# Three parts by turns instead of two for the first two token blocks of a fused recurrence and two-layer expert kernel

## The chip, the cores and the metric

The kernel runs on one core of a Trainium2 chip. The metric is the device time of one execution in microseconds. The engines are named as the profile names them: PE (matmul; PEld is its weight load), DVE (vector), ACT (scalar), POOL (GpSimd) and SP (which issues the transfers).

## The reference, cut to what matters

```python
# 1. a gated recurrence: 4 batches x 8 heads, 768 steps of time, head size 48
f = 1.0 / (1.0 + np.exp(-f_logit))
for t in range(S):
    state = f[:, :, t, :, None] * state + np.einsum('bhd,bhe->bhde', k[:, :, t], v[:, :, t])
    y[:, :, t] = np.einsum('bhd,bhde->bhe', q[:, :, t], state)
x = y.transpose(0, 2, 1, 3).reshape(B * S, H * D)     # 3072 tokens x 384

# 2. a product layer, d_ff = 1536
x = ((x @ w_a) * (x @ w_b)) @ w_out

# 3. four experts, F = 1024 each, weighted by p = domain_probs / sum
out = sum(p[:, e:e+1] * (np.maximum(x @ w1[e], 0) @ w2[e]) for e in range(4))
```

The three weight matrices of layer 2 reach the kernel as 64-bit floats; the kernel turns them into 32-bit ones on the chip.

## The kernel before

The 3072 tokens are cut into six **blocks** of 512 (four batches x 128 steps of time). The work has two phases. Phase A does the recurrence and the product layer, phase B the four experts.

**The recurrence** goes in 24 **steps** s (four per block; block i needs steps 4i to 4i+3). A step loads q, k, f and v (`a_load`), prepares them (`a_exp`, `a_scan`, `a_inv`, `a_hat`), and then does transposes, scores and output on PE (`a_trans`, `a_scores`, `a_out`). For steps below `EARLY` (8 before) `a_inv` does nothing: `a_hat` takes 1/R as exp(-ln R) on ACT and refines it with two DVE instructions (L237, L239) and one on POOL (L238), and half of the score mask goes to ACT and POOL (L275, L276). From `EARLY` on the reciprocal is four DVE instructions a step (L215). `a_out` writes the tokens into `xT[i]`, of which there are two buffers (pool `xp`), and after every second step six small transfers move rows inside `xT` (L338). The tiles of a step share `SLOTS` = 11 buffers.

**The product layer** of a block goes over 12 **column blocks** f of `w_a` and `w_b` (128 columns each). A **unit** (i, o, n, f, fs) is one column block for n tokens of block i from column o: two groups of nine matmuls (`half`, L358), an ACT copy (L486), a DVE product (L491 or L494), and then, after the two groups of the next unit, its share of the output product (`outp`). In the first `WHOLE` units the output product is three full 32-bit matmuls (L369); in the others the operands are split into a high and a low part by ACT and POOL (by ACT and DVE from unit `LATE` = 20 on) and nine matmuls follow (L376). A run of units over the column blocks `fs` collects in three banks, which are emptied into `x2raw` at its end: copied in the first run of a block (L391, L393), added by DVE in a later one (L389).

**The order of units.** `parts` cuts the 12 column blocks into 0 to 8 and 9 to 11 (`H1` = 9). Block 0 takes the first part, then block 1 takes it, then block 0 and block 1 take the second; blocks 2 to 5 take all 12 at once. Block 0 starts with four units of 256 tokens, so there are 74 units: unit 4 is block 0's f = 2, units 5 to 10 its f = 3 to 8, units 11 to 19 are block 1's first part, 20 to 22 block 0's second, 23 to 25 block 1's second, and block 2 begins at unit 26.

**The weights.** `conv_to(k)` makes sure that k of the 18 weight tiles of 128 x 768 are ready (two for each column block and one of `w_out` for each two). One conversion is an ACT instruction (L103), six DVE instructions (L104, L106, L109, L112, L113, L116) and, for 12 of the 18, a split by ACT and POOL (L122 on w). Before unit u the kernel calls `conv_to(w_units(min(NF, f + CA)))`, which is two column blocks ahead of the unit.

**Order.** The program text gives the priority; within phase A's first two blocks a planner orders each engine's instructions by that priority and by when they can start, and for blocks 2 to 5 PE keeps the order of the text. `goal` spreads the operations of the recurrence over the units: the steps of the next block are given out over the first `FRAC` (0.4) of the units that remain until that block, in blocks 0 and 1. Each engine runs its own queue in order, and SP issues every transfer in order.

Of the kernel before, what the change touches and what calls it, by code (L numbers as in the profile page):

```python
# [19 lines left out]
B, H, S, D = 4, 8, 768, 48  # L20
# [4 lines left out]
NF = 12  # L25
# [2 lines left out]
NB = 512  # L28
NBLK = NT // NB
HB = 256  # L30
EARLY = 2 * B

SLOTS = 11
FREE = 3 * B
# [2 lines left out]
AHEAD = 2  # L37
GRP = 2
BUSY = (8, 10, 8, 6)
H1 = 9  # L40
NSUB = 2
CA = 2
FRAC = 0.4
WHOLE = 8
LATE = 20
LIMIT = float(2.0 ** 60)

# [5 lines left out]
def gla_moe_moe_kernel(ctx: ExitStack, tc, qkf, vv, wab, wout, w12, probs, gq, gv, gp, out):  # L53
# [65 lines left out]
    def split(engine, hi, lo, x):  # L119

        nc.scalar.copy(out=hi, in_=x)  # L121
        engine.tensor_tensor(out=lo, in0=x, in1=hi.bitcast(F32), op=ALU.subtract)  # L122

    def x2_split(n, pool, tag, bufs):
        t = pool.tile([128, 2, KC, NB], F32R, tag=tag, name="x2", bufs=bufs)
        r = x2raw.pop(n)
        for o in range(0, NB, HB):
            split(nc.gpsimd, t[:, 0, :, o:o + HB], t[:, 1, :, o:o + HB], r[:, :, o:o + HB])
        x2[n] = t


    def phase_a(actx):
# [12 lines left out]
        def w_fetch(u):  # L145
            f, i = 2 * (u // 3), u % 3
            raws[u] = fetch_w(wout[f // 2] if i == 1 else wab[f + i // 2])

        def w_ready(u):
            f, i = 2 * (u // 3), u % 3  # L150
            raw = raws.pop(u)
            if i == 1:
                dst = wo_all[:, f:f + 2].rearrange("p f c -> p (f c)")
                if wide:
                    to_f32(raw, dst)
                else:
                    nc.scalar.copy(out=dst, in_=raw)
                return
            f += i // 2
            w = to_f32(raw) if wide else raw  # L160
            if f == 0:
                w_pair[0] = wts.tile([128, 2, 2, 2 * DM], F32R, tag="x", name="w01", bufs=1)
            t = w_pair[0][:, f] if f < 2 else wts.tile([128, 2, 2 * DM], F32R, tag="w", name="w")
            split(nc.gpsimd, t[:, 0], t[:, 1], w)
            w_f[f] = t.rearrange("p a (i k c) -> p a i k c", i=2, k=KC)
# [18 lines left out]
        def slot(name):  # L184
            return at.tile([128, 4, C], F32, tag="t", name=name, bufs=SLOTS)
# [27 lines left out]
        def a_inv(s, j):  # L213
            if s >= EARLY:
                nc.vector.reciprocal(out=T[s]["f"][:, j], in_=T[s]["R"][:, j])  # L215

        def a_hat(s):
# [6 lines left out]
            j1 = at.tile([128, 4, C], BF16, tag="j", name="j")  # L224
            if s >= EARLY:
                nc.gpsimd.tensor_tensor(out=k, in0=k, in1=R, op=ALU.mult)  # L226
# [32 lines left out]
        def a_scores(s):  # L259
# [12 lines left out]
            for h in range(2):  # L272
                m = slot("ss")
                if h and s < EARLY:
                    nc.scalar.copy(out=m.rearrange("p j c -> p (j c)"), in_=sps[h])  # L275
# [14 lines left out]
        def a_out(s):  # L290
# [50 lines left out]
            if not last:  # L341
                new = at.tile([128, 4, D], F32, tag="st", name="st", bufs=B + 1)
                uv = ups[:, :4 * D].rearrange("p (j e) -> p j e", j=4)
                pe = t["pe"].to_broadcast([128, 4, D])
                sign = 1.0 if s >= EARLY else -1.0
                if c:
# [6 lines left out]
        def half(i, o, n, f, which):  # L353
            p = bank("h")[:, :n]
            x, w = xT[i], w_f[f]
            ops = [(w[:, a, which, k], x[:, q, k, o:o + n]) for k in range(KC) for a, q in ((0, 0), (0, 1), (1, 0))]
            for m, (l, r) in enumerate(ops):
                kept(nc.tensor.matmul(p, l, r, start=m == 0, stop=m == len(ops) - 1))  # L358
            return p
# [3 lines left out]
        def outp(i, o, n, f, fs, w, hl):  # L363
            if (i, fs[0]) not in x2ps:
                x2ps[i, fs[0]] = [bank("o") for _ in range(KC)]
            banks = x2ps[i, fs[0]]
            for m in range(KC):
                if w is None:
                    nc.tensor.matmul(  # L369
                        banks[m][:, o:o + n], wo_all[:, f, m * 128:(m + 1) * 128], hl,  # L370
                        start=f == fs[0] and o == 0, stop=f == fs[-1], skip_group_check=True,
                    )
                    continue
                for q, (a, b) in enumerate(((0, 0), (0, 1), (1, 0))):

                    kept(nc.tensor.matmul(  # L376
                        banks[m][:, o:o + n], w[:, a, m * 128:(m + 1) * 128], hl[:, b],
                        start=f == fs[0] and q == 0 and o == 0, stop=f == fs[-1] and q == 2, skip_group_check=True,
                    ))
            if f != fs[-1]:  # L380
                return
            old = x2raw.get(i)
            if old is None:
                x2raw[i] = keep.tile([128, KC, NB], F32, tag="k", name="x2raw")
            for c in range(o, o + n, HB):
                for m in range(KC):
                    dst, p = x2raw[i][:, m, c:c + HB], banks[m][:, c:c + HB]
                    if old is not None:
                        nc.vector.tensor_tensor(out=dst, in0=p, in1=dst, op=ALU.add)  # L389
                    elif m == 1:  # L390
                        nc.vector.tensor_copy(out=dst, in_=p)  # L391
                    else:
                        nc.scalar.copy(out=dst, in_=p)  # L393
# [6 lines left out]
        NW = 3 * NF // 2  # L400
        fetch, ready = list(range(NW)), list(range(NW))

        def conv_to(k):

            while len(ready) > max(0, NW - k):
                w_ready(ready.pop(0))
                if fetch:
                    w_fetch(fetch.pop(0))

        def w_units(f):  # L410
            return 3 * (f // 2) + (0, 2)[f % 2]
# [29 lines left out]
        def attn_to(k):  # L441
            nonlocal done
            while done < min(k, len(ops)):
                ops[done]()
                done += 1
# [10 lines left out]


        full = list(range(NF))
        parts = [full[:H1], full[H1:]]
        order = [(i, fs) for fs in parts for i in range(2)] + [(i, full) for i in range(2, NBLK)]  # L460
        units = [(i, 0, NB, f, fs) for i, fs in order for f in fs]
        units = [(0, o, HB, f, parts[0]) for o in (0, HB) for f in parts[0][:NSUB]] + units[NSUB:]
# [7 lines left out]
        for k in range(upto[0]):  # L470
            attn_to(k + 1)
            conv_to(int(3 * (k + 1) / upto[0]))
        prev = None
        for u, (i, o, n, f, fs) in enumerate(units):
            conv_to(w_units(min(NF, f + CA)))
            fixed[0] = i >= 2
            here = done
            u0 = max(m for m in marks if m <= u)
            u1 = min([m for m in marks if m > u], default=None)
            goal = upto[u0]  # L480
            if u1 is not None:
                part = 1.0 if u + 1 >= u1 else min(1.0, (u - u0 + 1) / ((FRAC if i < 2 else 0.9) * (u1 - u0)))
                goal += int(part * (upto[u1] - upto[u0]))
            pa = half(i, o, n, f, 0)
            a = g.tile([128, n], F32, tag="a", name="a")
            nc.scalar.copy(out=a, in_=pa)  # L486
            attn_to((here + goal + 1) // 2)
            pb = half(i, o, n, f, 1)
            if u < WHOLE:
                hl, w = g.tile([128, n], F32, tag="hl", name="hl", bufs=2), None  # L490
                nc.vector.tensor_tensor(out=hl, in0=pb, in1=a, op=ALU.mult)  # L491
            else:
                ab = g.tile([128, n], F32, tag="ab", name="ab")
                nc.vector.tensor_tensor(out=ab, in0=pb, in1=a, op=ALU.mult)  # L494
                hl = g.tile([128, 2, n], F32R, tag="hl", name="hl", bufs=2)
                split(nc.vector if u >= LATE else nc.gpsimd, hl[:, 0], hl[:, 1], ab)
                w = g.tile([128, 2, DM], F32R, tag="wo", name="wo", bufs=2)
                split(nc.vector if u >= LATE else nc.gpsimd, w[:, 0], w[:, 1], wo_all[:, f])
            attn_to(goal)
            if prev is not None:  # L500
                outp(*prev)
            prev = (i, o, n, f, fs, w, hl)
            if u == len(units) - 8:
                x2_split(0, wts, "x", 1)
# [221 lines left out]
    with ExitStack() as actx:  # L726
        phase_a(actx)
# [75 lines left out]
```

## Time and profile before

| | us |
|---|---|
| median of three runs (1414.99 to 1416.28) | 1416.1 |
| the profiled execution | 1415.95 |
| its span, first to last instruction | 1414.2 |
| PE busy in the span | 1381.6 |
| DVE busy in the span | 583.2 |
| ACT busy in the span | 392.9 |
| POOL busy in the span | 191.3 |

Around the span lie 1415.95 - 1414.2 = 1.75 us. Times in the rows below count from the start of the span. A busy PE is one that has a matmul in its pipe, not one at its full rate.

### The profile page before, as it was taken

What the parts mean: (1) busy time and instruction counts of PE and PEld (TensorE: products, weight loads), DVE (VectorE), ACT (ScalarE), POOL (GpSimd) and SP (SyncE); (2) the same over time, 40 slices, a digit from 0 to 9 for tenths busy, and PEclk for the clock granted to TensorE, in tenths of its full rate; (3) what the DMA queues carried; (4) which work ended last, traced back from release to release, by engine and by line L of the source; (5) the groups of instructions that cost most, each with busy time, mean ns of one, the idle gap of its engine ahead of it and who ended that gap; (6) DMA issues with size and microseconds to landing.
All of it is one profiled execution on the core that took longest, in us unless ns stands there. A gap on an engine that the chain in (4) does not pass through costs nothing.

```text
span 1414.2 us, 18060 instructions
## 1 busy us (share of the span) xinstructions
PE 1381.6 (98%) x7599; PEld 1190.7 (84%) x7599; DVE 583.2 (41%) x880; ACT 392.9 (28%) x733; POOL 191.3 (14%) x128
## 2 busy tenths in 40 slices
PE   7889999999999999999999999999999999999998
PEld 4676787888888878889999989999989999989997
DVE  7899716856565654432222222222222222222222
ACT  6453334433333324341111211111311112111111
POOL 4334431100000002360000310000300002100000
PEclk9889999999999999999999999999999999999999
DMA  6544101222121101200000200000200001000001
GB/s 232 168 156 147 53 0 44 67 65 57 32 66 45 56 17 35 68 23 0 1 1 0 68 23 1 0 1 1 89 1 0 1 0 45 1 23 23 23 23 47
DMA packets 28168, 60.27 MB, mean 43 GB/s; under 512 B 4016, under 2 KB 9392, under 8 KB 28080
## 3 DMA queue, kind: packets, MB, share of 16 engines
q1 hardware_dynamic: 28080, 59.05, 13.3%
q8 instruction: 61, 1.00, 0.3%
q14 instruction: 27, 0.22, 0.0%
HBM read 51.95 MB, written 4.72 MB: 40 GB/s over the span
## 4 chain that ended last, share of the span: by engine, by line


## 5 line engine op out<-in xcount | busy, mean ns | idle before, releaser
L545 PE MATMUL bank<-w,h 128*128 128x384 f32 x2304 | 411.3, 335 | 0.0
L545 PEld LDWEIGHTS bank<-w,h 128*128 128x128 f32 x2304 | 402.8, 188 | 5.0
L527 PE MATMUL bank<-x,w 128*128 128x512 f32 x1728 | 404.8, 390 | 0.0
L527 PEld LDWEIGHTS bank<-x,w 128*128 128x128 f32 x1728 | 323.3, 188 | 65.2
L530 DVE SCALAR_TENSOR_TENSOR h<-bank,h 128x512 fp32r<-128x512 f32 x192 | 132.7, 691 | 533.1 <-ACT h L529 533.1
L358 PE MATMUL bank<-xT,w 128*128 128x512 f32 (+1 forms) x1332 | 319.1, 390 | 3.4 <-DVE ab L494 1.6
L358 PEld LDWEIGHTS bank<-xT,w 128*128 128x128 f32 x1332 | 246.2, 190 | 57.7 <-DVE ab L494 2.4
L529 ACT ACTIVATE h<-bank 128x512 fp32r<-128x512 f32 x192 | 114.9, 598 | 616.0 <-PE bank L527 516.7
L376 PE MATMUL bank<-hl,wo 128*128 128x512 f32 x594 | 148.9, 394 | 1.6 <-DVE hl L122 1.1
L122 POOL TENSOR_TENSOR w<-raw,w 128x768 fp32r<-128x768 f32 x32 | 59.0, 1844 | 575.6 <-ACT w L121 573.6
L376 PEld LDWEIGHTS bank<-hl,wo 128*128 128x128 f32 x594 | 109.9, 188 | 27.3 <-DVE hl L122 1.8
L494 DVE TENSOR_TENSOR ab<-bank,a 128x512 f32<-128x512 f32 x66 | 45.0, 682 | 132.7 <-PE bank L358 132.7
L121 ACT CAST hl<-ab 128x512 fp32r<-128x512 f32 x66 | 40.9, 620 | 83.5 <-DVE ab L494 83.5
L555 DVE SCALAR_TENSOR_TENSOR acc<-bank,pr,acc 128x384 f32<-128x384 f32 x72 | 39.5, 610 | 58.6 <-PE bank L545 58.6
L486 ACT COPY a<-bank 128x512 f32<-128x512 f32 (+1 forms) x74 | 42.1, 569 | 70.0 <-PE bank L358 70.0
L122 DVE TENSOR_TENSOR hl<-ab,hl 128x512 fp32r<-128x512 f32 x54 | 49.4, 914 | 28.6 <-ACT hl L121 28.6
L215 DVE RECIPROCAL f<-R 128x128 f32<-128x128 f32 x64 | 57.6, 926 | 0.7
L226 POOL TENSOR_TENSOR k<-k,R 128x512 f32<-128x512 f32 x16 | 22.0, 1373 | 265.6 <-DVE R L209 247.0
L121 ACT CAST wo<-wo_all 128x384 fp32r<-128x384 f32 x66 | 33.9, 515 | 40.0 <-PE bank L376 39.2
L122 DVE TENSOR_TENSOR wo<-wo_all,wo 128x384 fp32r<-128x384 f32 x54 | 34.4, 637 | 19.1 <-ACT wo L121 19.0
L121 ACT CAST w<-raw 128x768 fp32r<-128x768 f32 x32 | 26.8, 837 | 44.7 <-PE bank L545 30.8
L266 PE MATMUL bank<-q,k 48*128 48x128 f32 x320 | 25.6, 296 | 6.5 <-DVE q L239 5.8
(106 smaller groups left out, 773.0 us busy)
## 6 DMA issues: line engine op xcount, KB each, us to landing
raw<-in_w_dram SPq DMA_DIRECT2D x32, 384.0 KB, 3.0
raw<-in_wab_dram SPq DMA_DIRECT2D x12, 768.0 KB, 4.9
f<-in_qkf_dram SPq DMA_DIRECT2D x20, 256.0 KB, 2.7
k<-in_qkf_dram SPq DMA_DIRECT2D x20, 256.0 KB, 2.7
q<-in_qkf_dram SPq DMA_DIRECT2D x20, 256.0 KB, 2.8
v<-in_v_dram SPq DMA_DIRECT2D x20, 256.0 KB, 3.0
raw<-in_wout_dram SPq DMA_DIRECT2D x6, 768.0 KB, 4.4
out_dram<-acc SPq DMA_DIRECT2D x24, 192.0 KB, 1.9
```

What stands on the lines that cost most here:

```text
L121: nc.scalar.copy(out=hi, in_=x)
L122: engine.tensor_tensor(out=lo, in0=x, in1=hi.bitcast(F32), op=ALU.subtract)
L215: nc.vector.reciprocal(out=T[s]["f"][:, j], in_=T[s]["R"][:, j])
L358: kept(nc.tensor.matmul(p, l, r, start=m == 0, stop=m == len(ops) - 1))
L376: kept(nc.tensor.matmul(banks[m][:, o:o + n], w[:, a, m * 128:(m + 1) * 128], hl[:, b], start=f == fs[0] and q == 0 and o == 0, stop=f == ...
L486: nc.scalar.copy(out=a, in_=pa)
L494: nc.vector.tensor_tensor(out=ab, in0=pb, in1=a, op=ALU.mult)
L527: nc.tensor.matmul(p, l, r, start=i == 0, stop=i == len(ops) - 1)
L529: nc.scalar.activation(out=h[:, 0], in_=p, func=AF.Relu)
L530: nc.vector.scalar_tensor_tensor(out=h[:, 1], in0=p, scalar=0.0, in1=h[:, 0].bitcast(F32), op0=ALU.max, op1=ALU.subtract)
L545: nc.tensor.matmul(src, h[:, b, t * 128:(t + 1) * 128], w2[e, f][:, a], start=f == 0 and q == 0, stop=f == NF2 - 1 and q == 2,)
L555: nc.vector.scalar_tensor_tensor(out=dst, in0=src, scalar=p, in1=dst, op0=ALU.mult, op1=ALU.add)
```

## The change

The two first blocks take the column blocks in three parts of four by turns (block 0, block 1, block 0, and so on); the weight conversions are called one unit ahead of need, and from unit 6 on at an even pace that ends at unit 15 (`last` = 16); the steps of block 2 are prepared like the early ones; the first six units, not eight, have the full 32-bit output product; and the steps of the next block are spread over 0.9 of the units that remain until it (0.7 while the unit is block 1's). The units become: 0 to 5 block 0's f = 0 to 3 (four of them with 256 tokens), 6 to 9 block 1's f = 0 to 3, 10 to 13 block 0's f = 4 to 7, 14 to 17 block 1's, 18 to 21 block 0's f = 8 to 11, 22 to 25 block 1's. Block 2 still begins at unit 26, and there are still 74 units.

```diff
-EARLY = 2 * B
+EARLY = 3 * B
...
-H1 = 9
+PART = 4
 NSUB = 2
-CA = 2
-FRAC = 0.4
-WHOLE = 8
+FRAC = (0.9, 0.7, 0.9)
+WHOLE = PART + NSUB
 LATE = 20
...
-        parts = [full[:H1], full[H1:]]
+        parts = [full[f:f + PART] for f in range(0, NF, PART)]
...
+        second = WHOLE
+        last = second + PART + NF // 2
+
+        def pace(u):
+            k0 = w_units(PART)
+            return k0 + int((NW - k0) * min(1.0, (u + 1 - second) / (last - second))) if u >= second else 0
+
         prev = None
         for u, (i, o, n, f, fs) in enumerate(units):
-            conv_to(w_units(min(NF, f + CA)))
+
+            conv_to(max(w_units(1 + max(x[3] for x in units[:u + 2])), pace(u)))
...
-                part = 1.0 if u + 1 >= u1 else min(1.0, (u - u0 + 1) / ((FRAC if i < 2 else 0.9) * (u1 - u0)))
+                part = 1.0 if u + 1 >= u1 else min(1.0, (u - u0 + 1) / (FRAC[min(i, 2)] * (u1 - u0)))
```

## Rows read from the trace of the kernel before

**Rows 1.** Windows: busy us (instructions) of each engine, PE clock, DMA share, GB/s.

```profile
0.00:52.20 52.20, 42.55 (x330) 25.61 (x331) 41.48 (x63) 30.53 (x62) 21.96 (x23) 0.97 0.62 223
52.20:111.85 59.65, 51.21 (x394) 42.55 (x393) 56.39 (x76) 31.73 (x66) 23.95 (x17) 0.80 0.47 146
111.85:187.97 76.12, 71.21 (x348) 53.57 (x346) 59.13 (x76) 28.54 (x54) 34.28 (x23) 1.00 0.27 84
187.97:232.31 44.34, 43.49 (x191) 35.24 (x189) 12.31 (x20) 14.43 (x27) 11.83 (x10) 1.00 0.00 1
232.31:263.98 31.67, 30.95 (x270) 25.13 (x269) 30.56 (x57) 16.06 (x38) 3.87 (x3) 1.00 0.40 105
263.98:546.00 282.02, 281.14 (x1755) 229.62 (x1754) 163.32 (x268) 102.96 (x217) 14.20 (x11) 1.00 0.16 46
```

**Rows 2.** Timeline of PE: start, us, instructions [idle before <- releaser].

```profile
181.85 4.24 PE L358 MATMUL bank<-xT,w 128*128 128x512 f32 x18
185.93 2.20 PE L376 MATMUL bank<-hl,wo 128*128 128x512 f32 x9
```

**Rows 3.** Groups by line of DVE, 0 to 109.6 us: busy us, mean ns | idle before.

```profile
L109 DVE SCALAR_TENSOR_TENSOR cv<-raw,cv 128x768 uint32<-128x768 uint32 x10 | 12.1, 1205 | 0.0
L113 DVE SCALAR_TENSOR_TENSOR cv<-raw,cv 128x768 f32<-128x768 uint32 x9 | 9.2, 1027 | 0.0
L104 DVE TENSOR_SCALAR cv<-cv 128x768 f32<-128x768 f32 x10 | 8.1, 811 | 0.4 <-ACT cv L103 0.4
L112 DVE TENSOR_SCALAR cv<-cv 128x768 uint32<-128x768 uint32 x10 | 8.0, 804 | 0.0
L106 DVE TENSOR_SCALAR cv<-cv 128x768 uint32<-128x768 uint32 x10 | 7.5, 755 | 0.1
L237 DVE SCALAR_TENSOR_TENSOR q<-q,f 128x512 f32<-128x512 f32 x4 | 6.6, 1647 | 0.0
...
L116 DVE TENSOR_TENSOR cv<-cv 128x768 f32<-128x768 f32 x6 | 6.0, 1000 | 0.0
...
L239 DVE SCALAR_TENSOR_TENSOR q<-R,q 128x512 f32<-128x512 f32 x4 | 2.7, 678 | 0.0
```

**Rows 4.** Timeline of DVE: start, us, instruction.

```profile
108.47 0.68 DVE L491 TENSOR_TENSOR hl<-bank,a 128x512 f32<-128x512 f32 x1
...
110.02 0.55 DVE L104 TENSOR_SCALAR cv<-cv 128x768 f32<-128x768 f32 x1
...
112.19 0.69 DVE L331 TENSOR_TENSOR xT<-bank,xT 128x512 fp32r<-128x512 f32 x1 [0.76 <-ACT xT L330]
...
186.23 0.69 DVE L494 TENSOR_TENSOR ab<-bank,a 128x512 f32<-128x512 f32 x1 [5.43 <-PE bank L358]
```

**Rows 5.** Timeline of SP: start, us, transfers issued.

```profile
113.59 3.78 SPq L338 DMA_DIRECT2D xT<-xT  x6
```

**Rows 6.** Transfers by tile: count, KB each, median us from issue to landing.

```profile
xT<-xT SPq DMA_DIRECT2D x72, 32.0 KB, 2.0
```

**Rows 7.** Groups by line of DVE, 110 to 177 us.

```profile
L215 DVE RECIPROCAL f<-R 128x128 f32<-128x128 f32 x8 | 7.4, 933 | 0.0
...
L229 DVE TENSOR_TENSOR q<-q,f 128x512 f32<-128x512 f32 x2 | 2.5, 1232 | 0.0
L230 DVE COPY pe<-f 128x4 f32<-128x4 f32 x2 | 2.2, 1109 | 0.0
```

**Rows 8.** Groups by line and form of DVE, whole span.

```profile
L389 DVE TENSOR_TENSOR x2raw<-bank,x2raw 128x256 f32<-128x256 f32 x12 | 4.5, 412 | 0.0
```

**Rows 9.** Groups by line and form of POOL, 0 to 177 us.

```profile
L122 POOL TENSOR_TENSOR hl<-ab,hl 128x512 fp32r<-128x512 f32 x5 | 7.8, 1568 | 12.7 <-ACT hl L121 12.7
L122 POOL TENSOR_TENSOR wo<-wo_all,wo 128x384 fp32r<-128x384 f32 x6 | 7.2, 1208 | 5.7 <-ACT wo L121 5.7
L276 POOL TENSOR_SCALAR_AFFINE_SELECT ss<-ss 128x512 f32<-128x512 f32 x8 | 7.2, 896 | 20.2 <-DVE ss L282 9.4 <-ACT ss L275 6.8 <-DVE wo_all L116 4.0
...
L238 POOL TENSOR_TENSOR R<-R,f 128x512 f32<-128x512 f32 x4 | 6.0, 1500 | 5.4 <-ACT f L233 5.4
```

## The prediction

> **What bounds the kernel now.** I began with the windows [rows 1], cut where units begin: unit 6 at 111.85, unit 16 at 187.97, unit 26 (block 2) at 263.98. From 187.97 on PE is the limit. In the last window, the first 282 us from block 2 on, it is busy for 281.14 of 282.02 us, and the change touches nothing there except that block 2 starts from another time. The reader should see that only the first three windows have time to give, and that in them the engine that is full is DVE: 56.39 of 59.65 us and 59.13 of 76.12 us. From 52.2 to 111.85 PE's clock was granted at 0.80 on average, a mixture of 1.2 and 2.4 GHz; from 111.85 on it is 2.4 GHz throughout.
>
> Next the timeline of PE [rows 2]: a full-size unit at full speed goes from 181.85 to 187.97, 6.12 us for its 27 matmuls (18 and 9). Ten of them are 61.2 us. Units 6 to 15 took 76.1, of which PE shows 71.2 busy [rows 1]: the 10 us above 61.2 are step 8's matmuls and matmuls that were held up inside their groups. PE's own need lies between 61.2 and 71.2; I take 67, nearer the upper end because a step's matmuls are real work. The slack there is 9 us. Before it the slack is larger: units 1 to 5 and steps 4 to 7 fill 59.65 us, in which PE waited for 8.4 us and ran at the lower clock for part of the rest.
>
> Then the groups of DVE up to 109.6 us [rows 3]. One conversion is six instructions: 1.205 + 1.027 + 0.811 + 0.804 + 0.755 + 1.0 = 5.6 us; the ends of such rows overlap the next ones' starts, and I take off 0.5 us for that: 5.1 us net (single lines can be shorter: L104 at 110.02 takes 0.55 [rows 4]). Nine conversions are complete by then and a tenth is begun. Nine times 5.1 is 46 us, about half of all that DVE did. Unit 5's product, L491 at 108.47 [rows 4], stands behind all of them.
>
> **The change, part by part.**
>
> *Weights later.* By unit 5's product the text now asks for 6 conversions, where 9 were done: three fewer, 15.3 us of DVE. If DVE is all that holds steps 4 to 7 and units 2 to 5, that product comes 15.3 us earlier. If what holds them is the chain of a step (load, exp, scan, ln, exp, POOL, scores, mask, output, through 11 shared buffers), it comes no earlier. DVE idled for 3.3 us in that window [rows 1], so I stand near the upper end, and give back 4 us, since conversions also fill the gaps in the chains: 11 us earlier, at 97.5.
>
> *Block 1 right after unit 5.* Before, unit 11 was the first to read `xT[1]`, long after the last write to it at 112.19. Now unit 6 is. It has to wait for step 7's output, the six transfers behind it (3.78 us to issue [rows 5]) and the landing (2.0 us [rows 6]), 5.8 us in all. The output products of units 4 and 5 can cover 2 to 4 us; without that cover the whole 5.8 shows on PE. Step 7's L331 came 3.7 us after L491 of unit 5, so unit 6 starts near 97.5 + 3.7 + 0.7 + 5.8 = 107.7 against 111.85. DVE does not stand still in this wait: conversions 7 and 8 are next in the text.
>
> *Units 6 to 15.* Here DVE gets more, not less. Between the products of units 5 and 15 (108.47 and 186.23 [rows 4]) it was busy for about 62 us: 59.13 [rows 1] and 3 us before the window. I change that sum:
> - 12 conversions instead of 8 (17 were done by then, 18 will be): + 4 x 5.1 = + 20.4.
> - Steps 8 and 9 without reciprocals, L229 and L230: - 7.4 - 2.5 - 2.2 = - 12.1 [rows 7]; with two of L237 (1.65) and L239 (0.68) [rows 3]: + 4.7.
> - Two more ends of parts: block 1's first is copied (0.8 on DVE, the same as for block 0's), block 0's second is added, 6 x 0.412 [rows 8] = 2.5: + 3.3.
> - More for POOL: units 6 and 7 are now split (hl 1.57 and wo 1.21, twice: 5.6), two of L238 (3.0), two masks (1.8), 10.4 us [rows 9]. What does this cost DVE? L104 has taken 0.55 [rows 4] and averages 0.81 [rows 3], so DVE pays already. It pays between 0 and the whole 10.4. The three single-input lines of a conversion alone (L104, L112, L106) lost ten times 0.26, 0.25 and 0.20, 7.1 us up to 109.6, while POOL was busy for 46 us [rows 1]; with the two-input lines about twice that. I take a third: + 3.5.
>
> The sum is 62 + 20.4 - 12.1 + 4.7 + 3.3 + 3.5 = 81.8 us. PE's own need, from 107.7, ends unit 15's two groups at about 107.7 + 67 - 2 = 173. So DVE sets the pace: 97.5 + 81.8 = 179.3 for unit 15's product, against 186.23. The gain is 7 us. On paper the conversions that PE needs last (column blocks 8 to 11) could wait until unit 18; the even pace puts them ahead of unit 15's product in DVE's queue, so some of what the first part wins is given back here.
>
> A rule of the Trainium skill speaks against the change at this place: SBUF — State Buffer, section "SBUF: two separate sides", says that DVE and GpSimd share a port pair as an exclusive lock, held for the full instruction, and that the loser fully blocks. The lengthened L104 and L112 [rows 3] agree with it in kind. If every added POOL microsecond blocked DVE for as long, the item would be 10.4 instead of 3.5 and the time 1415, no change.
>
> *ACT and the whole-to-split units.* Two units go from six full 32-bit matmuls to nine split ones, a small saving for PE in a stretch that DVE paces: nothing. ACT gets an ln, an exp and a mask copy per step of block 2, and two casts for each of two units; it was busy for 28.5 of 76 us [rows 1], and DVE's pace covers it. If that cover went, ACT's added instructions, each shorter than a unit, would lie between PE's groups one at a time.
>
> *Units 16 to 25.* They start from 2.4 GHz and a free DVE. In the two windows between 187.97 and 263.98 PE is busy for 43.5 + 31.0 = 74.4 of 76.0 us [rows 1]. Conversion 18 no longer falls here and block 0's input buffer is released one unit earlier, with four units of block 1 behind it for cover instead of three. I take 1 of the 1.6 us that PE waited. The two other new adds (5 us of DVE) lie beside a DVE that was busy for 12 of 44 us.
>
> *Phase A's rest and phase B* start earlier by the same amount and keep it: PE is the limit there.
>
> Sum: 1415.95 - 7 - 1 = 1407.95, so **1408 us**. The profiled execution lies 0.15 us below the median of the runs shown, so the sum stands for it too. Smaller differences than 0.2% (2.8 us) can't be told from no change with this kernel.
>
> **Rivals.**
>
> *The steps' own chains hold units 2 to 5 (no change).* Unit 5's product stays near 108.5, step 7 ends as before, and unit 6 waits for the shuffle until 113 + 5.8 = 119, 7 us later than before. DVE uses the time for conversions, as before, and is ahead; PE then sets the pace: 119 + 67 = 186 to 188 for unit 16, against 187.97. Result 1414 to 1416. For it: four steps share 11 buffers. Against it: DVE was busy for 95% of this window.
>
> *DVE falls behind in units 6 to 15 (slower).* One mechanism: POOL's work and the even pace meet, and a conversion costs more than it did. The sum holds 5.1 us net and 3.5 us for POOL, 5.4 a conversion; the 8 us of gain are gone at 5.4 + 8/12 = 6.1. If all six instructions lose as much again as L104 now loses (0.26), a conversion costs 5.1 + 1.56 = 6.7, which is 12 x 1.3 = 15 us over the sum: about 1423. For it: POOL gets the splits of all ten units and two preparations, and L230, a copy of four elements, averages 1.1 us [rows 7], so it was held. Against it: POOL was busy for less than half of that stretch.
>
> *PE, not DVE, sets the pace of units 6 to 15 (more gain).* If the conversions lose nothing to POOL (5.1 - 0.7 = 4.4 us), DVE is done 12 x 0.7 + 3.5 = 12 us sooner than summed, at 167, and unit 16 starts at PE's pace, 107.7 + 67 = 175, 13 us early: 1402 with the last item. If PE's own work also covers most of the shuffle, so that unit 6 starts at 103, it is 1397. For it: L104 can take 0.55 [rows 4]. Against it: POOL was busy for 34 of the 76 us [rows 1], and gets more.
>
> **How the numbers follow.** Forecast (1403 to 1413): 0.50. More gain (1395 to 1403): 0.14. No change (1413.3 to 1418.9): 0.20. Slower: 0.16. Faster by over 0.2% is the first two with a little of their edges: 0.64; same 0.20; slower 0.16. The range drops the far end of the slower case and of the larger gain: 1399 to 1420.
>
> **What would show it.** Right: L491 of unit 5 near 97 with six to seven conversions behind it; a wait of PE for the shuffle before unit 6; DVE full until about 179; unit 16 near 180; block 2's first unit 8 us before 263.98; no L215 for steps 8 to 11. Wrong: steps 4 to 7 end near 109 as before, unit 16 at or after 188, conversions above 6.1 us net, or PE waiting at the ends of parts for an add. A new wait after unit 16, at block 2's inputs for instance, would break the last item.

## The result and the profile after

The changed kernel takes 1427.87 us (median of 4 runs, 1427.04 to 1431.06) against 1416.02 beside it: a ratio of 1.0088, 95% interval 1.0076 to 1.0099. It is slower by 0.9%, where 1408 and a gain were forecast. The profiled execution is one of 1427.04 us with a span of 1425.3, 11.1 us above the span before. In the changed code the lines ahead of the list of units have numbers one lower than before (conversion: L102, L103, L105, L108, L111, L112, L115; split: L120 on ACT, L121), a product is L498 or L501 instead of L491 or L494.

The windows of the changed kernel, cut at the same places as [rows 1]:

```profile
0.00:52.20 52.20, 43.16 (x300) 25.81 (x301) 43.00 (x63) 32.12 (x65) 22.94 (x24) 0.93 0.60 217
52.20:111.85 59.65, 52.06 (x442) 41.07 (x440) 45.91 (x70) 33.47 (x74) 27.34 (x18) 0.91 0.41 121
111.85:187.97 76.12, 63.10 (x316) 48.98 (x314) 70.31 (x77) 30.67 (x53) 38.45 (x24) 0.98 0.31 107
187.97:232.31 44.34, 44.00 (x192) 35.94 (x194) 19.77 (x33) 14.87 (x27) 15.92 (x13) 0.96 0.00 1
232.31:263.98 31.67, 29.75 (x242) 23.97 (x239) 22.34 (x41) 17.52 (x39) 10.17 (x8) 0.89 0.36 112
263.98:546.00 282.02, 281.14 (x1755) 229.58 (x1754) 162.54 (x268) 101.95 (x213) 14.20 (x11) 1.00 0.15 45
```

DVE's work has moved from the second window (45.91 us busy instead of 56.39) to the third (70.31 instead of 59.13), and in the third PE loses 8 us: 63.10 instead of 71.21. The last row is as before, so the loss lies ahead of it. The first matmuls of units show where:

| unit | before | changed kernel | later by |
|---|---|---|---|
| 6 | 111.85 | 110.88 | -1.0 |
| 10 | 141.53 | 142.04 | 0.5 |
| 16 | 187.97 | 194.15 | 6.2 |
| 22 | 226.42 | 231.39 | 5.0 |
| 26 (block 2) | 263.98 | 274.62 | 10.6 |

There are two losses, some 7 us from unit 6 to 16 and 5.7 from unit 22 to 26, and a gain of 1.2 between them.

**Units 6 to 16.** The steps with waits in PE's timeline show who is late:

```profile
134.73 2.37 PE L357 MATMUL bank<-xT,w 128*128 128x512 f32 x9 [1.65 <-DVE ab L501]
139.42 2.82 PE L375 MATMUL bank<-hl,wo 128*128 128x512 f32 x8 [2.10 <-POOL hl L121]
...
182.87 2.33 PE L357 MATMUL bank<-xT,w 128*128 128x512 f32 x9 [2.00 <-ACT a L493]
188.31 3.92 PE L357 MATMUL bank<-xT,w 128*128 128x512 f32 x9 [3.11 <-DVE ab L501]
```

A product L501 stands in DVE's queue behind conversions; the matmuls need the bank that it empties. The last row also shows the clock: nine matmuls in 3.92 us instead of 2.37, granted at half (1.2 GHz) from 188.4 to 191.8, after 2.00 and 3.11 us of waiting. It was also at half from 140.6 to 144.0, behind the waits of 1.65 and 2.10 us. Together that is 6.8 us at half clock, or 3.4 us of full-speed work.

DVE's groups from unit 5's product (100.84) to unit 15's (193.94), the lines of the conversion:

```profile
L108 DVE SCALAR_TENSOR_TENSOR cv<-raw,cv 128x768 uint32<-128x768 uint32 x11 | 18.4, 1674 | 0.2
L112 DVE SCALAR_TENSOR_TENSOR cv<-raw,cv 128x768 f32<-128x768 uint32 x10 | 11.8, 1176 | 0.2
L111 DVE TENSOR_SCALAR cv<-cv 128x768 uint32<-128x768 uint32 x11 | 11.3, 1030 | 0.2
L105 DVE TENSOR_SCALAR cv<-cv 128x768 uint32<-128x768 uint32 x11 | 8.6, 779 | 0.2
L103 DVE TENSOR_SCALAR cv<-cv 128x768 f32<-128x768 f32 x11 | 8.1, 739 | 2.3 <-ACT cv L102 2.1
```

Against [rows 3], L108 has gone from 1205 to 1674 ns and L111 from 804 to 1030. In the rest of the text "a conversion" is the sum of the six lines' means between the starts of units 6 and 16 (all six, L115 with them): 5.60 us before, 6.47 in the changed kernel. The windows of the rows shown differ a little from that stretch, and so do their means. And DVE was not full. Its waits in the same stretch (engine, line, waited for, us, times, longest):

```profile
DVE ab L501 <- POOL hl L121: 3.4, 1, 3.4
DVE cv L103 <- ACT cv L102: 2.1, 2, 1.5
DVE q L236 <- ACT f L232: 1.8, 1, 1.8
DVE pe L239 <- POOL R L237: 1.2, 1, 1.2
```

In all DVE was idle for 11.1 of these 93.1 us. Half of that lies before unit 6, beside the last early step, as its timeline shows:

```profile
103.34 0.69 DVE L236 SCALAR_TENSOR_TENSOR q<-q,f 128x512 f32<-128x512 f32 x1 [1.81 <-ACT f L232]
105.19 0.17 DVE L239 SCALAR_TENSOR_TENSOR pe<-R,f 128x4 f32<-128x4 f32 x1 [1.16 <-POOL R L237]
...
106.15 0.68 DVE L330 TENSOR_TENSOR xT<-bank,xT 128x512 fp32r<-128x512 f32 x1
...
107.74 0.76 DVE L390 COPY x2raw<-bank 128x256 f32<-128x256 f32 x2 [0.65 <-PE bank L368]
110.04 0.56 DVE L103 TENSOR_SCALAR cv<-cv 128x768 f32<-128x768 f32 x1 [1.55 <-ACT cv L102]
```

The eighth conversion begins only at 110.04; the seventh ended at 86.

**Units 22 to 26.** The window between these two units, of the changed kernel:

```profile
231.39:274.62 43.23, 41.31 (x293) 33.34 (x292) 26.83 (x48) 21.37 (x46) 10.21 (x8) 0.92 0.27 83
```

Before, the stretch took 37.56 us. In PE's timeline a wait is followed by matmuls at half the rate (16 of L302 take 1.08 us at 2.4 GHz):

```profile
237.56 0.90 PE L265 MATMUL bank<-q,k 48*128 48x128 f32 x6 [1.47 <-DVE q L238]
...
241.19 1.95 PE L302 MATMUL bank<-q,st 48*48 48x128 f32 x16
```

The half clock lasts from 239.6 to 246.4: 6.8 us, in which 3.4 us of full-speed work is lost. In this stretch the matmuls of steps 9 to 11 stand in PE's queue among those of unit 22, in the order that the planner chose, and PE runs its queue in order.

### The profile page after: what moved, and what is told of

Read it like the earlier page. It is cut to its first block, busy times and chain, and to the rows that moved or that the text cites. A ratio compares the mean times of both kernels' runs of the same rounds, so it can differ in the third digit from the quotient of the medians.

```text
span 1425.3 us, 18100 instructions
## 1 busy us (share of the span) xinstructions
PE 1385.0 (97%) x7605; PEld 1193.2 (84%) x7605; DVE 588.1 (41%) x876; ACT 403.1 (28%) x749; POOL 210.2 (15%) x140
## 4 chain that ended last, share of the span: by engine, by line
## 5 line engine op out<-in xcount | busy, mean ns | idle before, releaser
L357 PE MATMUL bank<-xT,w 128*128 128x512 f32 (+1 forms) x1332 | 318.1, 390 | 11.4 <-DVE ab L501 8.0
L375 PE MATMUL bank<-hl,wo 128*128 128x512 f32 x612 | 154.6, 396 | 4.5 <-POOL hl L121 3.4
L121 POOL TENSOR_TENSOR w<-raw,w 128x768 fp32r<-128x768 f32 x32 | 59.0, 1843 | 575.6 <-ACT w L120 573.5
L375 PEld LDWEIGHTS bank<-hl,wo 128*128 128x128 f32 x612 | 113.5, 188 | 31.5 <-POOL hl L121 4.7
L501 DVE TENSOR_TENSOR ab<-bank,a 128x512 f32<-128x512 f32 x68 | 46.4, 683 | 118.4 <-PE bank L357 111.3
L120 ACT CAST hl<-ab 128x512 fp32r<-128x512 f32 x68 | 42.1, 620 | 76.5 <-DVE ab L501 76.5
L121 DVE TENSOR_TENSOR hl<-ab,hl 128x512 fp32r<-128x512 f32 x54 | 49.7, 920 | 32.2 <-ACT hl L120 32.0
L493 ACT COPY a<-bank 128x512 f32<-128x512 f32 (+1 forms) x74 | 42.1, 569 | 66.8 <-PE bank L357 66.8
L225 POOL TENSOR_TENSOR k<-k,R 128x512 f32<-128x512 f32 x12 | 15.5, 1291 | 249.1 <-DVE R L208 247.9
L120 ACT CAST wo<-wo_all 128x384 fp32r<-128x384 f32 x68 | 34.7, 512 | 38.9 <-PE bank L375 38.5
L214 DVE RECIPROCAL f<-R 128x128 f32<-128x128 f32 x48 | 43.1, 926 | 0.7
L121 DVE TENSOR_TENSOR wo<-wo_all,wo 128x384 fp32r<-128x384 f32 x54 | 34.6, 640 | 19.3 <-ACT wo L120 19.3
L120 ACT CAST w<-raw 128x768 fp32r<-128x768 f32 x32 | 26.8, 837 | 44.7 <-PE bank L552 30.8
L309 PE MATMUL bank<-ss,v 128*64 128x128 f32 x320 | 26.4, 301 | 4.1 <-DVE ss L281 2.2
```

Of the source, the lines that this page charges most:

```text
L375: kept(nc.tensor.matmul(banks[m][:, o:o + n], w[:, a, m * 128:(m + 1) * 128], hl[:, b], start=f == fs[0] and q == 0 and o == 0, stop=f == ...
```

## The experiments

Three theories were set against each other. **A**: conversions are asked for too late, DVE stands idle before unit 6 and is behind from then on. **B**: the splits that units 6 to 15 now give POOL (units 6 and 7 newly) and its other work lengthen DVE's conversions. **C**: the early form of block 2's steps costs time where they stand, from unit 22 on. Times are medians, ratios are to the kernel before on the same chip with 95% intervals.

**e1_asked**, the conversions asked for sooner from unit 0 on:

```diff
-            conv_to(max(w_units(1 + max(x[3] for x in units[:u + 2])), pace(u)))
+            asked = (3, 5, 5, 5, 6, 8, 9, 11, 12, 14, 15)
+            conv_to(max(w_units(1 + max(x[3] for x in units[:u + 2])), asked[min(u, 10)]))
```

> The changed kernel with one thing put back: the conversions are asked for as early as in the kernel before (8 by unit 5, 15 by unit 10, the last three on need). Theory A (the conversions were moved out of DVE's idle time ahead of unit 6 into units 6 to 15, and the products wait behind them): DVE idles less than 6 us between 85 and 110, unit 16 starts near 182 to 186, and the time falls by 8 to 12 us to 1416 to 1420. Theory B (POOL's added work slows every conversion wherever it stands): the six lines still sum to 6.3 us or more a conversion and the time falls by less than 4 us. Theory C (the early form of steps 8 to 11 costs the time behind unit 22): its 5 to 6 us stay whatever happens before, so the time stays at 1420 or more.

1431.93 us, 1.0111 (1.0094 to 1.0128): 4 us more than the changed kernel. Nine conversions instead of seven are done by unit 5's product, which comes at 109.04 instead of 100.84; unit 6 starts at 119.05 instead of 110.88, and a conversion in units 6 to 16 still costs 6.61. A falls as a remedy: DVE's idle time before unit 6 was not free for the taking, conversions put there push the steps back.

**e2_early2**, the changed kernel with block 2's steps prepared as before:

```diff
-EARLY = 3 * B
+EARLY = 2 * B
```

> The changed kernel with the steps of block 2 prepared with reciprocals again. Theory C: the stretch from unit 22 to unit 26 falls from 43.2 to about 38 us and the time by 5 us to 1423, although DVE gets 3 us a step more before unit 16. Theory A: the stretch up to unit 16 gets 3 to 6 us longer, nothing comes back behind it, 1428 to 1434. Theory B: POOL loses two instructions of 1.5 us and two masks before unit 16, conversions fall by some 0.2 us each, 2 us less: about 1426.

1419.97 us, 1.0026 (1.0016 to 1.0036), 7.9 us under the changed kernel (5.6 us by the spans of the profiled runs). Units 6, 16, 18 and 22 start within 0.1 us of the changed kernel's; then comes the window from unit 22 to 26:

```profile
231.43:269.20 37.77, 36.86 (x293) 30.10 (x292) 31.68 (x57) 16.85 (x39) 4.08 (x3) 1.00 0.34 95
```

DVE does 5 us more here, and it costs nothing: it is busy for 31.68 of 37.77 us and the clock is 2.4 GHz throughout. C holds.

**e3_need**, the changed kernel without the even pace (`conv_to` by need alone):

> The changed kernel without the even pace: each weight one unit ahead of its need and no earlier, so 12 conversions spread over units 9 to 20 instead of 6 to 15. Theory A in the form that the pace itself puts conversions ahead of products: DVE has room again in units 6 to 15, unit 16 near 182, time 1415 to 1420. If late conversions are only met later by PE (need comes at units 10 and 18 with a queue of conversions in front), unit 16 is earlier but units 18 to 21 wait, and the time stays within 3 us of 1428. Theory B: no change of the sum of the six lines where POOL splits stand beside them; where DVE does the splits (unit 20 on) they are shorter.

1426.05 us, 1.0073 (1.0057 to 1.009). Unit 16 starts at 185.35, 8.8 us sooner than with the pace, but PE then waits in units 17 and 18 for products (L501) that stand behind the late conversions (unit 22 at 230.41 against 231.39). The pace only chose where DVE's lateness shows.

**e4_before_early3**, the kernel before with `EARLY = 3 * B`:

> The kernel before with only the steps of block 2 prepared like the early ones. Theory C: the stretch behind unit 22 gets 3 to 6 us longer, 1419 to 1422. Theory A: that form is not to blame, DVE has 12 us less to do by unit 16 and the time stays at 1413 to 1416. Theory B: two more POOL instructions for each of steps 8 and 9 beside the conversions, 0 to 2 us slower.

1420.78 us, 1.0032 (1.0019 to 1.0044): block 2's early form alone costs 4.6 us, without any other part of the change. In the profiled runs units 22 to 26 take 40.58 us at full clock, 3.0 more than before, and another 1.9 us are lost between units 6 and 16.

**e5_whole16**, as e2, with the full 32-bit output product up to unit 15, so that POOL splits nothing for these units:

```diff
-EARLY = 3 * B
+EARLY = 2 * B
...
-WHOLE = PART + NSUB
+WHOLE = 16
...
-        second = WHOLE
+        second = PART + NSUB
```

> The changed kernel with reciprocals for block 2 (1420) and the full 32-bit output product in the first 16 units, so that ACT and POOL split nothing for units 6 to 15; PE pays about 0.57 us a unit, 5.7 us. Theory B (POOL's splits hold DVE's conversions): the six lines between 108 and 197 us fall from 6.5 to 5.3 us or less a conversion, units 6 to 15 from 83 to 74 to 78 us, and the time to 1411 to 1415. Theory A (it is the number of conversions in this stretch, not POOL): conversions stay above 6 us and the time rises to 1421 to 1426.

**1409.22 us**, 0.9957 (0.9941 to 0.9974): faster than both kernels. Its DVE groups in the window of units 6 to 16 (108 to 197 us):

```profile
L108 DVE SCALAR_TENSOR_TENSOR cv<-raw,cv 128x768 uint32<-128x768 uint32 x11 | 13.5, 1229 | 0.2
L112 DVE SCALAR_TENSOR_TENSOR cv<-raw,cv 128x768 f32<-128x768 uint32 x11 | 11.0, 1001 | 0.2
L105 DVE TENSOR_SCALAR cv<-cv 128x768 uint32<-128x768 uint32 x11 | 7.6, 695 | 0.2
L111 DVE TENSOR_SCALAR cv<-cv 128x768 uint32<-128x768 uint32 x11 | 7.5, 684 | 0.2
L498 DVE TENSOR_TENSOR hl<-bank,a 128x512 f32<-128x512 f32 x10 | 6.8, 680 | 0.0
...
L103 DVE TENSOR_SCALAR cv<-cv 128x768 f32<-128x768 f32 x11 | 6.1, 553 | 0.3 <-ACT cv L102 0.2
```

The same eleven conversions cost 5.13 us each (6.12 in e2), and unit 16 starts at 180.10. The windows between units 6 and 16, of e2 and of e5:

```profile
110.94:194.17 83.23, 71.73 (x336) 55.58 (x334) 81.01 (x94) 31.91 (x56) 39.78 (x25) 0.92 0.28 99
108.72:180.10 71.38, 69.11 (x309) 47.39 (x307) 69.25 (x95) 25.08 (x41) 15.60 (x9) 1.00 0.33 115
```

The stretch is 11.9 us shorter and DVE's busy time 11.8 us, 10.9 of it in the conversions. e2 also runs at half clock for 13.6 us of this stretch and e5 for none of it, but DVE is idle for only 2.2 and 2.1 us of it, so the difference is DVE's work and hardly the clock. A full output product is longer on PE (a unit 6.68 us instead of 6.12), and it is the faster kernel all the same.

**e6_light**, as e2, but from the seventh weight tile on the conversion is one ACT copy of the high words (so these weights are not the reference's):

> The changed kernel with reciprocals for block 2, and from the seventh weight tile on the conversion left out: ACT copies one half of each 64-bit word and DVE does none of its six instructions, so the output is not the reference's. Theories A and B (DVE's conversions set the pace of units 6 to 15): the stretch falls to PE's own need, 67 to 70 us, unit 16 starts near 180 and the time is 1403 to 1408. If something else holds these units (the shuffle before unit 6, banks, POOL's splits by themselves): unit 16 stays above 188 and the time above 1413.

1405.66 us, 0.9931 (0.9911 to 0.9951), unit 16 at 178.11. This is what the stretch takes when DVE has no conversions, though POOL still does its splits (33.7 us): the splits hurt through DVE, not by themselves.

**e7_pace20**, as e2 with the even pace drawn out to unit 19 (`last = 20`):

> The changed kernel with reciprocals for block 2 and the even pace drawn out to unit 19 instead of 15: 12 conversions over 14 units, each still a unit or more ahead of its need. Theory A: DVE's load falls from 1.2 to 0.86 conversions a unit, 6.0 to 6.7 us with the product, near PE's 6.1, so units 6 to 15 take 72 to 76 us, unit 22 starts near 225 and the time is 1412 to 1416. If the total of DVE's work up to unit 20 is what counts and not its pace, unit 22 stays near 230 and the time at 1418 to 1421.

1420.77 us, 1.0038 (1.0024 to 1.0052). Unit 16 at 185.90, 8.3 us sooner than in e2, unit 22 at 231.14 as in e2. Like e3: the sum of DVE's work decides.

**e8_before_ca1**, the kernel before with weights asked for one column block ahead (`CA = 1`):

> The kernel before with its conversions one column block ahead instead of two, nothing else. If conversions ahead of need hold steps 4 to 7 and units 2 to 8 (the first term of the prediction, without the new order): unit 6 starts 3 to 6 us earlier and the time is 1411 to 1413. If the chains of the steps hold them, or DVE does the same work later in front of other products: unit 6 within 2 us of 111.85 and the time within 3 us of 1416.

1424.18 us, 1.0059 (1.0042 to 1.0075). Unit 6 stays at 111.13; the planner still puts nine conversions ahead of unit 5's product, so the run does not test that term of the prediction. Unit 16 starts 3.2 us sooner, but PE waits for late weights behind unit 20 (ACT's split of w, 3.8 us at one place), and in the old order the later request is a loss.

**e9_poolonly**, as e5, with idle work on POOL: four subtractions of the product, 128x224, into a tile that nothing reads:

```diff
+        idle = g.tile([128, 224], F32, tag="idle", name="idle")
...
+                if u >= 6:
+                    for c in (0, 64, 128, 192):
+                        nc.gpsimd.tensor_tensor(out=idle, in0=hl[:, c:c + 224], in1=hl[:, 224:448], op=ALU.subtract)
```

> The kernel of the run with 16 full products and reciprocals (1409), plus four POOL subtractions of 128x224 for each of units 6 to 15 (about 2.4 us, as much as the two splits took) whose result nobody reads. Theory B (POOL working beside DVE lengthens the conversions, whoever needs POOL's result): the six lines go from 5.1 back to 6 us or more, units 6 to 15 from 71 to 80 us or more, and the time to 1418 to 1422. If the splits cost by their own latency in front of the output product (ACT, POOL, then PE): conversions stay below 5.4 us and the time at 1408 to 1412.

1424.72 us, 1.0062 (1.0045 to 1.0079): 15.5 us come back, more than the 9 to 13 expected; POOL is busy for 51.9 us between units 6 and 16, where e2's splits made it 39.8. DVE's groups, same stretch:

```profile
L108 DVE SCALAR_TENSOR_TENSOR cv<-raw,cv 128x768 uint32<-128x768 uint32 x11 | 15.5, 1412 | 0.2
L112 DVE SCALAR_TENSOR_TENSOR cv<-raw,cv 128x768 f32<-128x768 uint32 x11 | 14.3, 1304 | 0.2
L103 DVE TENSOR_SCALAR cv<-cv 128x768 f32<-128x768 f32 x11 | 8.6, 786 | 2.9 <-ACT cv L102 2.8
...
L499 DVE TENSOR_TENSOR hl<-bank,a 128x512 f32<-128x512 f32 x10 | 6.8, 679 | 0.0
```

A conversion costs 6.10 us, and no instruction of DVE waits for POOL (its waits there are 2.8 us for ACT and 1.8 for PE). DVE is busy for 80.66 us between units 6 and 16, 11.4 more than in e5; the stretch is 16.3 longer, and the other 4.9 are idle time. One instruction shows how it comes about. POOL's timeline has

```profile
146.76 2.27 POOL L121 TENSOR_TENSOR w<-cv,w 128x768 fp32r<-128x768 f32 x1
```

and DVE's, in the same execution,

```profile
147.28 1.78 DVE L229 COPY pe<-f 128x4 f32<-128x4 f32 x1
148.97 0.68 DVE L499 TENSOR_TENSOR hl<-bank,a 128x512 f32<-128x512 f32 x1
```

Four elements a partition are copied in 1.78 us, and the copy ends at 149.06, 0.03 us after POOL's instruction at 149.03. In e5 the same copy has a free POOL:

```profile
140.76 0.16 DVE L229 COPY pe<-f 128x4 f32<-128x4 f32 x1
```

**e10_before_whole16**, the kernel before with `WHOLE = 16`:

> The kernel before with the full 32-bit output product in the first 16 units instead of 8, nothing else. Theory B: its conversions between units 6 and 16 fall from 5.6 to 5.2 us or less, the stretch from 76 to 72 to 74 us (PE pays 4.6 us for eight units and sets the pace), time 1411 to 1415. If the three parts by turns are what made 1409 possible, it stays at 1414 or more; if not, it comes to 1409 to 1411.

1416.96 us, 1.0008 (0.9998 to 1.0017). A conversion falls to 5.20, POOL to 15.2 us, and nothing is gained: between units 6 and 16 PE is busy for 73.98 of 76.15 us with the longer units. In the old order PE was the limit as soon as DVE was relieved.

**e11_mask**, the changed kernel with only the mask of block 2's steps as before (`if h and s < 2 * B` in `a_scores`):

> The changed kernel, where the steps of block 2 keep the early preparation but mask both halves of the scores on DVE again. If the mask's way over ACT and POOL makes their chains long: the stretch from unit 22 to 26 falls from 43 to 39 us or less and the time to 1422 to 1424. If it is exp(-ln R) with its POOL and DVE refinement: the stretch stays above 42 us and the time at 1426 to 1429.

1424.33 us, 1.006 (1.0043 to 1.0077), 3.5 us under the changed kernel. Its window from unit 22 to 26:

```profile
232.50:272.36 39.86, 37.12 (x293) 30.10 (x292) 28.70 (x51) 19.16 (x43) 6.85 (x5) 1.00 0.31 90
```

3.4 us shorter than the changed kernel's, and just the half clock is gone. The other 2 us against e2's 37.77 belong to the early preparation, and stay. So the window, at 39.86, fits neither forecast: the mask brings the larger part, the preparation the rest.

**e12_after_whole16**, the changed kernel with `WHOLE = 16` (and `second = PART + NSUB`), block 2's early form kept:

> The changed kernel with the full output product in the first 16 units and nothing else changed (the early form for block 2 stays). If the two costs add (POOL's splits 10.8, block 2's form 5.6 to 7.9): 1415 to 1418, unit 16 near 180, units 22 to 26 again 42 us or more. If the early form only hurts because DVE and POOL are crowded: 1409 to 1411.

1420.02 us, 1.0033 (1.0021 to 1.0044), 7.9 us under the changed kernel and 10.8 over e5, above both forecasts. By the profiled runs, 9.9 us apart, 5.6 are units 22 to 26 (43.53 against 37.94 us, with a half clock of 6.8 us again) and 4.1 lie ahead of unit 22, 0.8 of them ahead of unit 6. Why the form of block 2 costs anything so early was not tried and stays open.

**e13_actonly**, e9's idle work given to ACT:

```diff
-                        nc.gpsimd.tensor_tensor(out=idle, in0=hl[:, c:c + 224], in1=hl[:, 224:448], op=ALU.subtract)
+                        nc.scalar.copy(out=idle, in_=hl[:, c:c + 224])
```

> As the kernel with 16 whole units (1409.2), but from unit 6 to 15 the idle work per unit is four copies 128x224 on ACT into the tile that nothing reads, where the POOL version (four subtractions, 1424.7) had them on POOL. If it is POOL that lengthens DVE's instructions: conversions stay at 5.1 to 5.2 us, unit 16 within 2 us of 180.1, 1409 to 1412. Rival: any further reader of the product, or the later release of its buffer, holds DVE: 1417 to 1425, with DVE or PE waiting for the copies.

1410.68 us, 0.9965 (0.9952 to 0.9977). The lines that e9 lengthened are as in e5:

```profile
L108 DVE SCALAR_TENSOR_TENSOR cv<-raw,cv 128x768 uint32<-128x768 uint32 x11 | 13.5, 1227 | 0.2
L112 DVE SCALAR_TENSOR_TENSOR cv<-raw,cv 128x768 f32<-128x768 uint32 x11 | 11.0, 1002 | 0.2
...
L103 DVE TENSOR_SCALAR cv<-cv 128x768 f32<-128x768 f32 x11 | 6.1, 555 | 1.4 <-ACT cv L102 1.4
```

ACT does 11 us of added work in that stretch (35.96 us busy against 25.08), with the same readers of the same buffer. That is less than the 36 us that e9 gave POOL, but in e9 DVE never waited for POOL. It is POOL's work as such that lengthens DVE's, not a further reader or a buffer that comes free later. Instruction by instruction the changed kernel says the same: of its ten L103 between units 6 and 16, the five beside no POOL instruction took 0.55 to 0.57 us, the two wholly beside one 1.36 and 1.61. B is shown for units 6 to 16.

**e14_need16**, e5 without the even pace:

> As the kernel with 16 whole units (1409.2), without the even pace: the weights are converted only by the need of the next units. If the even pace is worth something once conversions are cheap: units 17 to 20 wait for late weights, as they did without the pace in the slower setting, and it is 1412 to 1416. Rival: the sum of DVE's work alone counts, and the place of the conversions does not: 1408 to 1410.

1413.72 us, 0.9983 (0.9973 to 0.9992). The pace is worth 4.5 us here, as forecast, though mostly at another place: units 13 to 15 start 3.8 to 5.5 us later without it, where PE waits 4.0 us for the splits of weights, and 2.6 us more are lost from unit 16 to 20. With POOL's splits beside the conversions, and block 2's early form (e3), it was worth nothing.

## Why the prediction was wrong, by its own steps

*Weights later*: product of unit 5 forecast at 97.5, measured at 100.84. Right in sign, 3.3 us too much. DVE was no longer full there: from 84 to 110.9 us it was busy for 15.15 of 26.9 us and waited 4.0 us for ACT's exponential (L236) and 3.3 for POOL's product R (L238, L239). This points to the early steps' own chains, the first rival's cause, as the new limit; no run took them apart.

*Block 1 right after unit 5*: unit 6 forecast at 107.7, measured at 110.88, with 1.46 us of waiting for the six transfers. Counted from unit 5's product the forecast was 10.2 us and the measured stretch 10.0. The sentence "DVE does not stand still in this wait" was wrong: see the rows from 103.34 to 110.04.

*Units 6 to 15* is the step that failed: "DVE sets the pace: 97.5 + 81.8". It took 81.8 us of DVE's work as the time from unit 5's product to unit 15's, which was 93.1. The windows of that stretch, of the changed kernel,

```profile
100.84:193.94 93.10, 78.28 (x405) 59.40 (x402) 81.98 (x98) 39.15 (x73) 44.33 (x28) 0.96 0.30 99
```

of e5,

```profile
101.18:179.34 78.16, 75.89 (x358) 51.38 (x355) 74.46 (x108) 29.86 (x53) 15.60 (x9) 1.00 0.35 118
```

and of the kernel before.

```profile
108.47:186.23 77.76, 72.85 (x374) 54.27 (x371) 61.40 (x81) 30.06 (x57) 35.78 (x23) 1.00 0.29 88
```

DVE's busy time is what the sum had, 81.98, but by luck, with two errors that cancel: eleven conversions instead of twelve (5.4 us less), each at 6.47 - 0.5 = 5.97 net instead of 5.4 (11 x 0.57 = 6.3 us more). What the sum left out is that busy time is not elapsed time: 93.10 - 81.98 = 11.1 us of DVE's idle time, some 5.5 before 110 and 3.4 for POOL's split of a product. The term "More for POOL: + 3.5" was the mis-sized one: a conversion went from 5.60 to 6.47 us, 11 x 0.87 = 9.6 us. And the item of steps 8 and 9 (12.1 us less, 4.7 more) bought no time: with reciprocals back (e2) DVE is busy for 3.7 us longer between units 6 and 16, and unit 16 starts at the same time. Nor did the sum have a term for the half clock. Taking POOL's splits of these units out (e5) gives conversions at 5.13 - 0.5 = 4.6 net, 3.7 us idle, and unit 15's product at 179.34. That the prediction had 179.3 is chance: e5 gets there from 101.18, not 97.5, and with 74.46 us of DVE work, not 81.8. The rival "DVE falls behind" named the mechanism, and 1423. But by its own point of decision (the gain is gone at 6.1 net) conversions of 5.97 would not have made the kernel slower; DVE's idle time and units 22 to 26, which it did not have, came on top.

The rule from the Trainium skill (SBUF — State Buffer, "SBUF: two separate sides") that the prediction weighed, an exclusive lock on the port pair with a loser that fully blocks, agrees in kind with the copy of 1.78 us. The prediction's reading of it, that every added microsecond of POOL could cost DVE one, is not what the runs show: 14.7 us more of conversions (11 x 1.34) beside 25.8 us more of POOL from e5 to the changed kernel, 10.7 (11 x 0.97) beside 36.3 from e5 to e9.

*ACT and the whole-to-split units* was costed at nothing, under the cover of DVE's pace. That cover was counted in busy time too: in the changed kernel PE waits between units 6 and 16 for 3.4 us in all for POOL's split of a product and for 2.0 us, once, for ACT's copy (L493).

*Units 16 to 25*: forecast a gain of 1 us. From unit 16 to 22 it came (37.24 us against 38.45), then units 22 to 26 lost 5.7: the early form of block 2's steps, which saves DVE work where DVE has time to spare, and adds waits to PE's queue, one of which was followed by 6.8 us at half clock. No rival had this, though the prediction's last sentence on signs names a new wait behind unit 16 as what would break the item. *Phase A's rest and phase B* are as forecast: PE is busy for 281.14 us of the last window in both kernels.

What the forecast saw in the three parts and the pace is there, once POOL's splits and block 2's early form are left out: with them 6.6 us are won (e5), and 2.5 without the pace (e14). The longer output product alone won nothing in the old order (e10), so the gain needs the new one. How the rest divides between the three parts, the later weights and the wider spread of the steps (`FRAC`) was not tried. The rival with more gain (1402) had conversions that lose nothing to POOL; e6, with none at all on DVE from the seventh on, came to 1405.66.

## What to carry to other kernels

A sum of busy times sets the pace of an engine only if its durations hold beside the new neighbours: before moving work to an "idle" POOL, price each line of DVE in stretches where POOL is busy and where it is not. An alternative that costs PE 0.56 us a unit was worth 10.8 us, because it took work from an engine that held up the bound one. And a form that saves work on an engine can be a loss in a stretch where that engine has time and another, which runs its queue in order, has to wait for the form's longer chain.

## What the runs showed of the hardware

Not every DVE instruction suffers beside POOL. The product with one operand from a matmul bank keeps its time (684 ns in the changed kernel, 680 in e5, 679 in e9); three of the ten between units 6 and 16 of the changed kernel lay wholly beside a POOL instruction and took 0.68 to 0.69 us like the others. By contrast L103, which has one operand and no bank, goes from 553 ns in e5 to 739 in the changed kernel and 786 in e9, and L108 with two from 1229 to 1674 and 1412. Not every line is longer in each run: L111 is at 1030 ns in the changed kernel, but at 641 in e9 against 684 in e5. In the changed kernel the clock fell to half at 140.6 for 3.4 us, after PE had waited for 1.65 and 2.10 us, at 188.4 for 3.4 us, after 2.00 and 3.11 us, and at 239.6 for 6.8 us, after 1.47 us of waiting among a step's small matmuls. In e5 a wait of 2.3 us between units 6 and 16 was not followed by it, and the clock held from 83 us to the end of phase A.
